# An attention-then-MLP kernel: the second quarter of the weights asked for earlier in the opening, and the order of the first layer's tiles changed to suit

## The chip, the cores and the metric

The kernel runs on one core of a Trainium2 chip. The time is device microseconds (us) of one execution; the median of five executions before the change is 203.65 us (202.69 to 204.04).

## What is computed

```python
# q, k, v: (4 batches, 8 heads, 768 steps, 64), fp32
gamma = 1.0 - 2.0 ** (-5.0 - np.arange(H))
for t in range(S):
    state = gamma[None, :, None, None] * state + np.einsum('bhd,bhe->bhde', k[:, :, t], v[:, :, t])
    y[:, :, t] = scale * np.einsum('bhd,bhde->bhe', q[:, :, t], state)
x = y.transpose(0, 2, 1, 3).reshape(3072, 512)
h = x @ w_in                      # w_in: 512 x 2048
g = gelu_tanh(h)
return g @ w_out                  # w_out: 2048 x 512
```

A decaying linear attention gives 512 features for each of 3,072 tokens; a two-layer MLP follows.

## The kernel before

**Tiling.** The 768 steps are cut into six chunks c of 128. A chunk has four batches b, so 512 tokens. Within a chunk the attention of a batch is made of matmuls: q and k, cast to fp16 and scaled (`prep1`, line 147), are transposed on TensorE (`mm_T`, 184) and evicted to qkT (`ev_T`, 193); scores are formed (`mm_A`, 203) and masked on VectorE (`ev_A`, 217); `mm_yc` and `mm_yi` (224, 239) form y, and `ev_Y` (252) writes it to xT, the MLP's input; `mm_s` and `ev_S` (261, 275) update the state st that chunk 1 needs. In chunk 0 `mm_yc` issues nothing.

**First layer (M1).** The 2,048 hidden features are 16 tiles fc of 128. `moe1` (372) computes one tile for all 512 tokens: four matmuls and one GELU on ScalarE. `moe1_two` (377) computes the pair fp, tiles 2fp and 2fp+1, for a stretch of tokens: t01 is batches 0 and 1, t2 batch 2, t3 batch 3. Each uses one of the two PSUM banks of the tag h, so a third has to wait for the GELU of the first. In chunk 0 the first layer starts before all batches are there; that is why pairs are computed stretch by stretch.

**Weights.** w_in is loaded in four parts of four tiles (`load_w_in`, 329): part 0 holds pairs 0 and 1, part 1 pairs 2 and 3, part 2 pairs 4 and 5, part 3 pairs 6 and 7. w_out comes in four parts too (`load_w_out`, 337). All are cast from fp32 to fp16 by the DMA and are issued from the queue of GpSimd (POOL in the profile).

**Second layer of chunk 0** (`units_0`, 614; its matmuls are lines 624 and 657). Products of g with w_out and of sums of both (`g_sums`, 402, and `w_sums`, 395, on VectorE), so it needs w_out parts as they come. Chunk 1's attention is woven in: after unit 3 ScalarE casts the first q and k rows of chunk 1, and after unit 5 TensorE transposes them.

**What sets the order.** The scheduling is manual. Each engine works through its own instructions in the order of the program text, and an instruction that has to wait holds up all behind it on that engine, DMA issues included. DMA issues stand on three queues: SP (`nc.sync`), ACT (`nc.scalar`) and POOL (`nc.gpsimd`). The rows of chunk 0 are issued from SP and ACT (lines 96 to 106, 717, 718, 726). POOL casts the k rows of chunk 0 and issues w_in, w_out and eight loads of chunk 1's rows:

```python
    prep1(PO, "k", 0, 0)          # 721
    load_w_in(0)                  # 722
    ...
    prep1(PO, "k", 0, 1)          # 728
    ...
    prep1(PO, "k", 0, 2)          # 740
    for i in range(1, 3):
        load_w_in(i)
    prep1(PO, "k", 0, 3)          # 743
    load_w_in(3)
```

`spin` (115) issues matmuls on zeros. The opening of chunk 0 is lines 717 to 801; line 787 is a one-element copy that keeps a later load behind w_out part 3, and `hold` (470) is another of the same kind.

Of the kernel before, what the change touches and what calls it, by code (L numbers as in the profile page):

```python
# [16 lines left out]
def kernel(  # L17
# [9 lines left out]
    nc = tc.nc  # L27
# [6 lines left out]
    NF = d_ff // 128  # L34
# [34 lines left out]
    misc = const.tile([128, 32], F32)  # L69
# [9 lines left out]
    def ld_tile(nm, c, b):  # L79
        if (nm, c, b) not in raw:  # L80
            tag, n = ("v1" if nm == "v" else "qk1", 5 if nm == "v" else 8) if c == 1 else (f"{nm}32", 4)
            raw[nm, c, b] = ld.tile([128, H, Dh], F32, tag=tag, bufs=n, name=f"{nm}32")
        return raw[nm, c, b]

    def load1(eng, nm, c, b):
        eng.dma_start(  # L86
            out=ld_tile(nm, c, b),
            in_=srcs[nm][b, :, c * C:(c + 1) * C, :].rearrange("h p d -> p h d"),
        )

    def load(c):
# [20 lines left out]
        out=misc[:, 0:1], in_=zero[:, 0:1], func=AF.Gelu_apprx_tanh, scale=1.0  # L112
    )

    def spin(n):
        ps = bank("h", shape=(128, 512), name="spin_ps")
        for _ in range(n):
            nc.tensor.matmul(
                out=ps, lhsT=zero[:, 0:128], rhs=zero, start=True, stop=True
            )  # L120


    st = const.tile([128, B, NHP, 2, 64], F16, name="st")
# [4 lines left out]
    for j in range(2):  # L128
        for hp in range(NHP):
            nc.vector.tensor_scalar(  # L130
                out=mask[:, j, hp],
# [9 lines left out]
    def copy_on(eng, out, in_):  # L141
        if eng is nc.scalar:
            eng.copy(out=out, in_=in_)  # L143
        else:
            eng.tensor_copy(out=out, in_=in_)

    def prep1(eng, nm, c, b):
        if nm == "v":
            t = pre.tile([128, H, Dh], F16, tag="v16", bufs=6, name="v16")
        else:  # L150
            if (c, b) not in qk16:
                qk16[c, b] = pre.tile([128, 2, H, Dh], F16, tag="qk16", bufs=6, name="qk16")
            t = qk16[c, b][:, "qk".index(nm)]
        src = ld_tile(nm, c, b)
        if (nm == "v") == (c < 1):
            copy_on(eng, t, src)
        else:
            col = OQ if nm == "q" else OK
            eng.tensor_tensor(  # L159
                out=t,  # L160
                in0=src,
                in1=cst[:, col:col + H].unsqueeze(2).broadcast_to([128, H, Dh]),
                op=ALU.mult,
            )
        h16[nm, c, b] = t
# [11 lines left out]
    def bank(tag, dt=F32, shape=(128, NHP, 128), name="ps"):  # L177
        return psum.tile(list(shape), dt, tag=tag, bufs=BANKS[tag], name=name)
# [5 lines left out]
    def mm_T(c, b):  # L184
        ps = bank("att", F16, (128, 2, NHP, 128), "qkT_ps")
        for i, nm in enumerate("qk"):
            for hp in range(NHP):
                nc.tensor.transpose(  # L188
                    out=ps[:, i, hp], in_=pair(h16[nm, c, b], hp), identity=iden
                )  # L190
        pss["T", c, b] = ps

    def ev_T(c, b, eng=nc.vector):
        copy_on(eng, qkT_tile(c, b), pss.pop(("T", c, b)))
# [8 lines left out]
    def mm_A(c, b):  # L203
        t = qkT[c, b]
        ps = [bank("att", name=f"a_ps{j}") for j in range(2)]
        for hp in range(NHP):
            for j in range(2):
                nc.tensor.matmul(  # L208
                    out=ps[j][:, hp],
                    lhsT=t[j * 64:(j + 1) * 64, 1, hp],  # L210
                    rhs=t[j * 64:(j + 1) * 64, 0, hp],
                    start=True,
                    stop=True,
                )
        pss["A", c, b] = ps

    def ev_A(c, b):
        ps = pss.pop(("A", c, b))
        for j in range(2):
            s = att.tile([128, NHP, 128], F16, tag=f"a{j}", bufs=2, name=f"a_sb{j}")  # L220
            nc.vector.tensor_tensor(out=s, in0=ps[j], in1=mask[:, j], op=ALU.mult)  # L221
            a_sb[c, b, j] = s
# [29 lines left out]
    def ev_Y(c, b, eng=nc.vector):  # L252
        if c not in xT:
            xT[c] = xp.tile([128, NHP, B * C], F16, tag="x", bufs=2, name="xT")
        x, ps = xT[c][:, :, b * C:(b + 1) * C], pss.pop(("Y", c, b))
        if c < 1:
            copy_on(eng, x, ps)
        else:
            nc.vector.tensor_tensor(out=x, in0=ps, in1=dec, op=ALU.mult)  # L259
# [15 lines left out]
    def ev_S(c, bs, engs=(nc.vector, nc.vector)):  # L275
        if c + 1 >= NCk:
            return
        s_ps = pss.pop(("S", c, bs))
        for j in range(2):
            sl = slice(j * 64, (j + 1) * 64)  # L280
            t = st[sl, bs[0]:bs[-1] + 1, :, j]
            if c == 0:
                copy_on(engs[j], t, s_ps[sl])
                continue
            for hp in range(NHP):
                nc.vector.scalar_tensor_tensor(  # L286
                    out=t[:, :, hp],
                    in0=t[:, :, hp],
                    scalar=cst[sl, OG + hp:OG + hp + 1],
                    in1=s_ps[sl, :, hp],  # L290
                    op0=ALU.mult,
                    op1=ALU.add,
                )
# [32 lines left out]
    NO = 4  # L326
    w_out_sb = [const.tile([128, NF // NO, d_model], F16, name=f"w_out{i}") for i in range(NO)]

    def load_w_in(i):
        nc.gpsimd.dma_start(  # L330
            out=w_in_sb[i],
            in_=moe_w_in.rearrange("(kc p) n -> p kc n", p=128)[
                :, :, w_in_at[i] * 128:(w_in_at[i] + w_in_n[i]) * 128
            ],
        )

    def load_w_out(i):
        n = NF // NO
        nc.gpsimd.dma_start(
            out=w_out_sb[i],  # L340
            in_=moe_w_out.rearrange("(fc p) n -> p fc n", p=128)[:, i * n:(i + 1) * n],
        )
# [4 lines left out]
    def moe1_mm(c, fc, out, t0, t1):  # L347
        wi, wr = w_in_of[fc]
        for kc in range(NHP):
            nc.tensor.matmul(  # L350
                out=out,
                lhsT=w_in_sb[wi][:, kc, wr * 128:(wr + 1) * 128],
                rhs=xT[c][:, kc, t0:t1],
                start=(kc == 0),
                stop=(kc == NHP - 1),
                skip_group_check=True,
            )

    def g_tile(c, fc):
        r = fc % 8 // 2 * 2  # L360
        return g_sb[fc // 8][:, r:r + 2]
# [7 lines left out]
    def gelu(out, in_):  # L369
        nc.scalar.activation(out=out, in_=in_, func=AF.Gelu_apprx_tanh, scale=1.0)  # L370

    def moe1(c, fc):
        h_ps = bank("h", shape=(128, B * C), name="h_ps")
        moe1_mm(c, fc, h_ps, 0, B * C)
        gelu(g_tile(c, fc)[:, fc % 2], h_ps)

    def moe1_two(c, fp, t0, t1):

        h_ps = bank("h", shape=(128, 2, B * C // 2), name="h_ps")
        for r in range(2):  # L380
            moe1_mm(c, 2 * fp + r, h_ps[:, r, 0:t1 - t0], t0, t1)
        gelu(g_tile(c, 2 * fp)[:, :, t0:t1], h_ps[:, :, 0:t1 - t0])
# [320 lines left out]
    def loads(eng, c, *what):  # L703
        for nm, b in what:
            load1(eng, nm, c, int(b))
# [7 lines left out]
    VE, AC, PO, SY = nc.vector, nc.scalar, nc.gpsimd, nc.sync  # L713
# [12 lines left out]
    load1(AC, "k", 0, 3)  # L726
    prep1(VE, "q", 0, 1)
    prep1(PO, "k", 0, 1)
    spin(2)
    mm_A(0, 0)  # L730
    ev_A(0, 0)
# [6 lines left out]
    ev_Y(0, 0, AC)  # L738
    prep1(VE, "q", 0, 2)
    prep1(PO, "k", 0, 2)  # L740
    for i in range(1, 3):
        load_w_in(i)
    prep1(PO, "k", 0, 3)
    load_w_in(3)
    for i in range(NO):
        load_w_out(i)
    loads(PO, 1, "q0", "k0", "q1", "k1", "v0", "v1", "q2", "k2")
    mm_A(0, 1)
    ev_A(0, 1)
    spin(2)  # L750
# [8 lines left out]
    mm_A(0, 2)  # L759
    ev_A(0, 2)  # L760
    ev_S(0, (0, 1), (AC, VE))
    prep1(VE, "q", 0, 3)

    t01, t2, t3 = (0, half), (half, half + C), (half + C, 2 * half)
# [2 lines left out]
    mm_yi(0, 2)  # L767
    ev_Y(0, 2, AC)
    moe1_two(0, 1, *t01)
    prep1(AC, "v", 0, 3)  # L770
    mm_T(0, 3)
    ev_T(0, 3)
    moe1_two(0, 0, *t2)
    moe1_two(0, 1, *t2)
    mm_A(0, 3)
    ev_A(0, 3)
    moe1_two(0, 2, *t01)
    mm_yc(0, 3, "o")
    mm_yi(0, 3)
    mm_s(0, (2, 3))  # L780
    ev_Y(0, 3)
    ev_S(0, (2, 3))
    moe1_two(0, 2, *t2)
    for fp in range(3):
        moe1_two(0, fp, *t3)

    nc.gpsimd.tensor_copy(out=dec[0:1, 0, 0:1], in_=w_out_sb[3][0:1, 0, 0:1])
# [1 line left out]
    loads(PO, 1, "q3", "k3", "v2", "v3")  # L789
    loads(SY, 2, *[x + str(b) for nm in ("qk", "v") for b in range(B) for x in nm])  # L790

    for fc in range(6, NF):
        moe1(0, fc)
        if fc == 7:
            g_sums(VE, 0, 0, 2)
            w_sums(0)
        if fc == 8:
            g_sums(VE, 0, 2, 4)
        if fc == 11:
            w_sums(1)  # L800
            g_sums(VE, 0, 4, 6)
# [262 lines left out]
```

## Time and profile before

| what | value |
|---|---|
| median of five runs | 203.65 us |
| time of the profiled execution | 203.65 us |
| its span, first to last instruction | 200.8 us |
| granted TensorE clock, mean | 0.992 |
| PE busy | 190.6 us, 95% of the span |
| DVE, ACT, POOL busy | 133.8, 119.0, 132.2 us |
| DMA | 34.24 MB, mean 171 GB/s |
| w_in parts 0 to 3: issue | 6.63, 11.87, 12.68, 17.94 us |
| w_in parts 0 to 3: landing | 14.93, 20.31, 22.85, 25.39 us |
| batch 3's q, k, v: landing | 16.12, 16.36, 17.17 us |
| w_out part 0: landing | 27.96 us |

PE is TensorE's matmuls and PEld its weight loads, DVE is VectorE, ACT ScalarE, POOL GpSimd, SP the sync engine; a q behind a name means its sequencer. L350 is line 350. Times in the trace count from the span's start. A wait row names the engine and line that waited, what ended the wait, and the total, the number and the longest of the waits. A timeline row has the start, the duration, the engine, the line, the operation, its output and inputs, and in brackets the idle time before it with what ended it. In the chain of work that ended last, each step is followed back to what released it, so it shows what set the pace; a DMA in it is a transfer from its issue to its landing. A DMA queue's row has packets, megabytes and the time of its packets as a share of 16 engines over the window.

### The profile page before, as it was taken

The numbers are of one execution on the slowest core, as the hardware profiler recorded it, in microseconds if no ns is written. First come the engines' busy times: TensorE is split into PE (matmuls) and PEld (weight loads), VectorE is DVE, ScalarE is ACT, GpSimd is POOL, SyncE is SP. The second block draws the span as 40 slices with busy tenths as digits, with TensorE's granted clock in tenths as the row PEclk, the third lists the DMA queues.
The fourth block names the chain that finished last, engine by engine and source line by source line (L and its number), as shares of the span: only waits on it lengthen the run. The fifth ranks groups of instructions, "written<-read, shape, count | busy, mean of one in ns | idle before, by whom it ended". The sixth has DMA issues, their size and how long they took to land.

```text
span 200.8 us, 5015 instructions
## 1 busy us (share of the span) xinstructions
PE 190.6 (95%) x2014; PEld 149.1 (74%) x2014; DVE 133.8 (67%) x279; ACT 119.0 (59%) x218; POOL 132.2 (66%) x134
## 2 busy tenths in 40 slices
PE   5588999999999999999999999999999999999993
PEld 1346746887888888745478887888888888888882
DVE  5356759869792449995997975995835935217720
ACT  2386474473589409265657698379584495867211
POOL 0557833845189998769969529389979299598100
PEclk9889999999999999999999999999999999999999
DMA  7999999999998799999999597531400220002204
GB/s 164 288 235 227 206 207 242 343 341 218 322 238 119 175 259 213 175 295 248 216 221 253 132 246 173 119 151 48 108 0 3 97 112 3 0 0 109 104 25 184
DMA packets 87094, 34.24 MB, mean 171 GB/s; under 512 B 80032, under 2 KB 84512, under 8 KB 87072
## 3 DMA queue, kind: packets, MB, share of 16 engines
q1 hardware_dynamic: 73920, 19.25, 45.0%
q0 software_dynamic: 6624, 12.58, 24.0%
q10 hardware_dynamic: 6528, 2.10, 4.1%
q8 instruction: 15, 0.25, 0.5%
q14 instruction: 7, 0.06, 0.1%
HBM read 27.63 MB, written 6.29 MB: 169 GB/s over the span
## 4 chain that ended last, share of the span: by engine, by line
PE 86%; DMA 8%; DVE 2%; SPq 1%; POOL 1%; issue 1%; ACT 0%; DVEq 0%
PE o_ps L504 31%; PE h_ps L350 19%; PE h_ps L586 19%; DMA w_in<-in_moe_w_in_dram 4%; DMA k<-in_k_dram 3%; PE y_ps L243 3%; PE o_ps L624 3%; PE a_ps L208 3%; PE o_ps L657 3%; PE y_ps L230 2%; PE s_ps L267 1%; SPq L86 1%; DVE a_sb L221 1%; PE qkT_ps L188 1%; DVE xT L259 1%; POOL qk L159 1%
## 5 line engine op out<-in xcount | busy, mean ns | idle before, releaser
L350 PE MATMUL h_ps<-xT,w_in 128*128 128x256 f16 (+2 forms) x304 | 45.9, 301 | 1.3 <-DMA w_in<-in_moe_w_in_dram 1.3
L370 ACT ACTIVATE g<-h_ps 128x512 f16<-128x512 f32 (+1 forms) x55 | 31.5, 577 | 20.4 <-PE h_ps L350 18.5
L221 DVE TENSOR_TENSOR a_sb<-a_ps,mask 128x512 f16<-128x512 f32 x48 | 30.5, 684 | 15.9 <-PE a_ps L208 13.3
L393 POOL TENSOR_TENSOR s_g<-g 128x512 f16<-128x512 f16 x30 | 35.2, 1180 | 7.5 <-ACT g L370 6.5
L350 PEld LDWEIGHTS <-w_in 128*128 128x128 f16 x304 | 26.5, 98 | 15.8 <-DMA w_in<-in_moe_w_in_dram 1.7
L504 PEld LDWEIGHTS <-s_g 128*128 128x128 f16 x320 | 30.7, 98 | 4.2 <-POOL s_g L393 0.3
L370 ACT ACTIVATE g<-h_sb 128x512 f16<-128x512 f32 x36 | 22.0, 634 | 17.4 <-DVE h_sb L393 17.0
L504 PE MATMUL o_ps<-t_w,s_g 128*128 128x256 f16 x240 | 29.4, 273 | 0.0
L393 DVE TENSOR_TENSOR h_sb<-h_ps,h_sb 128x512 f32<-128x512 f32 x36 | 22.9, 684 | 9.6 <-ACT h_sb L143 8.9
L159 POOL TENSOR_TENSOR v<-v,cst 128x512 f16<-128x512 f32 x20 | 20.6, 1046 | 5.4 <-DMA v<-in_v_dram 4.2
L504 PEld LDWEIGHTS <-g 128*128 128x128 f16 x208 | 20.2, 98 | 2.5
L393 POOL TENSOR_TENSOR s_g<-s_g,g 128x512 f16<-128x512 f16 x18 | 21.0, 1164 | 1.4
L393 POOL TENSOR_TENSOR s_g<-g,s_g 128x512 f16<-128x512 f16 x18 | 20.6, 1155 | 0.0
L586 PEld LDWEIGHTS <-t_in 128*128 128x128 f16 x192 | 18.0, 98 | 2.9
L143 ACT COPY h_sb<-h_ps 128x512 f32<-128x512 f32 x36 | 19.1, 598 | 1.3 <-PE h_ps L586 1.2
L504 PE MATMUL o_ps<-w_out,g 128*128 128x256 f16 x160 | 19.1, 273 | 0.0
L286 DVE SCALAR_TENSOR_TENSOR st<-st,cst,s_ps 64x128 f16<-64x128 f16 x64 | 18.2, 346 | 0.2
L586 PE MATMUL h_ps<-s_x,t_in 128*128 128x256 f16 x144 | 17.8, 273 | 0.0
L259 DVE TENSOR_TENSOR xT<-y_ps,dec 128x512 f16<-128x512 f32 x20 | 13.3, 684 | 5.4 <-PE y_ps L243 5.4
L586 PEld LDWEIGHTS <-w_in 128*128 128x128 f16 x144 | 14.1, 98 | 1.8
L143 ACT CAST qk<-q 128x512 f16<-128x512 f32 x20 | 12.6, 630 | 2.8 <-DMA q<-in_q_dram 2.8
L143 ACT CAST qk<-k 128x512 f16<-128x512 f32 x20 | 12.6, 630 | 0.1
(81 smaller groups left out, 263.2 us busy)
## 6 DMA issues: line engine op xcount, KB each, us to landing
out_dram<-o_sb POOLq DMA_DIRECT2D x10, 512.0 KB, 3.6
k<-in_k_dram SPq DMA_DIRECT2D x18, 256.0 KB, 4.5
q<-in_q_dram SPq DMA_DIRECT2D x18, 256.0 KB, 4.5
v<-in_v_dram SPq DMA_DIRECT2D x18, 256.0 KB, 4.4
w_in<-in_moe_w_in_dram POOLq DMA_DIRECT2D x4, 512.0 KB, 8.4
w_out<-in_moe_w_out_dram POOLq DMA_DIRECT2D x4, 512.0 KB, 11.9
q<-in_q_dram POOLq DMA_DIRECT2D x4, 256.0 KB, 11.0
k<-in_k_dram POOLq DMA_DIRECT2D x4, 256.0 KB, 9.5
```

What stands on the lines that cost most here:

```text
L143: eng.copy(out=out, in_=in_)
L159: eng.tensor_tensor(out=t, in0=src, in1=cst[:, col:col + H].unsqueeze(2).broadcast_to([128, H, Dh]), op=ALU.mult,)
L208: nc.tensor.matmul(out=ps[j][:, hp], lhsT=t[j * 64:(j + 1) * 64, 1, hp], rhs=t[j * 64:(j + 1) * 64, 0, hp], start=True, stop=True,)
L221: nc.vector.tensor_tensor(out=s, in0=ps[j], in1=mask[:, j], op=ALU.mult)
L243: nc.tensor.matmul(out=y_ps[j * 64:(j + 1) * 64, hp], lhsT=h16["v", c, b][:, 2 * hp + j], rhs=a_sb[c, b, j][:, hp], start=(c == 0), stop=True,
L259: nc.vector.tensor_tensor(out=x, in0=ps, in1=dec, op=ALU.mult)
L286: nc.vector.scalar_tensor_tensor(out=t[:, :, hp], in0=t[:, :, hp], scalar=cst[sl, OG + hp:OG + hp + 1], in1=s_ps[sl, :, hp], op0=ALU.mult, ...
L350: nc.tensor.matmul(out=out, lhsT=w_in_sb[wi][:, kc, wr * 128:(wr + 1) * 128], rhs=xT[c][:, kc, t0:t1], start=(kc == 0), stop=(kc == NHP - ...
L370: nc.scalar.activation(out=out, in_=in_, func=AF.Gelu_apprx_tanh, scale=1.0)
L393: eng.tensor_tensor(out=out, in0=in0, in1=in1, op=op)
L504: nc.tensor.matmul(out=po, lhsT=lhs(c, lk, fp, a), rhs=rhs(rk, fp), start=(new and fp == 0 and (last or a == 0)), stop=(stop and fp == NP ...
L586: nc.tensor.matmul(out=self.ps[G, k][:, p], lhsT=self.lhs(lk, 2 * G + p, kc), rhs=self.rhs(rk, kc), start=(new and p == 0 and kc == 0), st ...
```

## The change

It edits the opening of chunk 0 only.

- Part 1 of w_in is issued from POOL right behind the cast of batch 1's k.
- Parts 2 and 3 of w_in, the cast of batch 3's k, w_out and chunk 1's loads move down the POOL queue, behind a one-element copy that reads st after the state update of batches 0 and 1.
- On TensorE, pairs 0 to 3 (tiles 0 to 7) of M1 are computed on batches 0 to 2 around batch 3's transposes; before, only pairs 0 and 1 came ahead of batch 3's scores. Five pairs instead of three are then taken stretch by stretch, and six tiles instead of ten on all 512 tokens at once.
- VectorE's sums of g pairs and of w_out part 0 are placed behind tile 10 instead of tiles 7 and 8.

```diff
     prep1(VE, "q", 0, 1)
     prep1(PO, "k", 0, 1)
+    load_w_in(1)
     spin(2)
...
     prep1(VE, "q", 0, 2)
     prep1(PO, "k", 0, 2)
-    for i in range(1, 3):
-        load_w_in(i)
-    prep1(PO, "k", 0, 3)
-    load_w_in(3)
-    for i in range(NO):
-        load_w_out(i)
-    loads(PO, 1, "q0", "k0", "q1", "k1", "v0", "v1", "q2", "k2")
     mm_A(0, 1)
...
     ev_S(0, (0, 1), (AC, VE))
+    nc.gpsimd.tensor_copy(out=misc[0:1, 2:3], in_=st[0:1, 0, 0, 0, 0:1])
+    for i in range(2, 4):
+        load_w_in(i)
+    prep1(PO, "k", 0, 3)
+    for i in range(NO):
+        load_w_out(i)
+    loads(PO, 1, "q0", "k0", "q1", "k1", "v0", "v1", "q2", "k2")
     prep1(VE, "q", 0, 3)
...
     moe1_two(0, 1, *t01)
+    for fp in range(2):
+        moe1_two(0, fp, *t2)
+    for fp in range(2, 4):
+        moe1_two(0, fp, *t01)
     prep1(AC, "v", 0, 3)
     mm_T(0, 3)
     ev_T(0, 3)
-    moe1_two(0, 0, *t2)
-    moe1_two(0, 1, *t2)
+    for fp in range(2, 4):
+        moe1_two(0, fp, *t2)
     mm_A(0, 3)
     ev_A(0, 3)
-    moe1_two(0, 2, *t01)
+    moe1_two(0, 4, *t01)
     mm_yc(0, 3, "o")
     mm_yi(0, 3)
     mm_s(0, (2, 3))
     ev_Y(0, 3)
     ev_S(0, (2, 3))
-    moe1_two(0, 2, *t2)
-    for fp in range(3):
+    moe1_two(0, 4, *t2)
+    for fp in range(5):
         moe1_two(0, fp, *t3)
...
-    for fc in range(6, NF):
+    for fc in range(10, NF):
         moe1(0, fc)
-        if fc == 7:
+        if fc == 10:
             g_sums(VE, 0, 0, 2)
             w_sums(0)
-        if fc == 8:
             g_sums(VE, 0, 2, 4)
```

## The prediction

> **What bounds the kernel now.** I read the 40 slices first: PE is at 9 tenths from slice 8 to the last, so nothing outside the first 40 us can be won here, and the question is how much PE idles in the opening. The waits of PE between 13 and 33 us answer it:
>
> ```profile
> PE h_ps L350 <- DMA w_in<-in_moe_w_in_dram: 1.3, 2, 0.7
> PE qkT_ps L188 <- POOL qk L159: 0.5, 1, 0.5
> ```
>
> The columns are total us, times, longest. The first wait for w_in (0.65 us, at 14.97) is for part 0, which the change leaves alone. That leaves 0.69 us for part 1 (until 20.36) and 0.48 us for the cast of batch 3's k (until 18.05): 1.17 us in all can be removed.
>
> Then the chain that ended last, in order of time:
>
> ```profile
> 3.98 6.72 DMA k<-in_k_dram
> ...
> 10.76 1.11 POOL qk L159
> 11.87 8.44 DMA w_in<-in_moe_w_in_dram
> ...
> 20.36 1.05 PE h_ps L350 x8
> ...
> 23.63 9.26 PE h_ps L350 x48
> 32.90 5.24 PE o_ps L624 x48
> 38.14 0.45 PE qkT_ps L188 x8
> ```
>
> Up to 20.3 us the chain is DMA, behind it PE without a break. The timeline shows what stands close behind PE at 38 us, the casts on ACT of the first rows of chunk 1:
>
> ```profile
> 36.35 0.62 ACT L143 CAST qk<-q 128x512 f16<-128x512 f32 x1 [2.82 <-DMA q<-in_q_dram]
> ...
> 37.11 0.62 ACT L143 CAST qk<-k 128x512 f16<-128x512 f32 x1
> ...
> 37.97 0.61 PE L188 MATMUL qkT_ps<-iden,qk 128*128 128x128 f16 x8
> ```
>
> ACT starts each cast as the row lands (36.33, 37.09). The k cast ends at 37.73; PE's four transposes of k run at about 38.2. So if PE came earlier, it would stop here: with k ready at 37.73 and 0.3 us for the four, this step can end at 38.1 at best instead of 38.58. **The gain is capped at about 0.5 us** unless those rows land earlier. They cannot: in windows of 2 us the DMA share is 1.21 to 1.28 from 6 to 34 us without a hole and 1.02 to 1.06 on larger packets to 40 us, and the change removes no byte.
>
> How the queues share the engines, from 10.9 to 11.7 us:
>
> ```profile
> q0 software_dynamic: 159, 0.16, 121.7%
> q10 hardware_dynamic: 29, 0.01, 4.0%
> q1 hardware_dynamic: 2, 0.00, 0.5%
> ```
>
> and from 12.5 to 13.5 us:
>
> ```profile
> q0 software_dynamic: 138, 0.14, 82.8%
> q1 hardware_dynamic: 139, 0.04, 26.9%
> q10 hardware_dynamic: 116, 0.03, 13.1%
> ```
>
> The columns are packets, MB, share. q0 is POOL's (w_in, 512 packets of 1 KB a part), q1 is SP's and q10 ACT's (rows, 1,024 packets of 256 B each). First the weights alone at 200 packets a us, then nearly equal packet counts, so four times the bytes for w_in. From 14 to 15 us the rows alone move at 1,100 packets a us.
>
> **Part 1 of w_in moved ahead: where it lands.** POOL ends the cast of k1 at 9.12 and issues part 1 there (0.81 us, to 9.93) instead of at 11.87. The cast of k2 starts when k2 lands (10.69), so that issue costs nothing on POOL: it lies in a wait of 1.64 us. What it does at the engines is the open question. The Trainium skill ("DMA: Bandwidth & Descriptors", Queues, rings and completion order) says that each DMA engine goes round the queues that have work, packet by packet, and this speaks against the change: with 1 KB against 256 B, a second part of w_in takes most bytes from batch 3's rows. The 12.5 row agrees with it. But another row does not: part 0 was issued at 6.63, and between 7.6 and 10.5 no packet of q0 moved; an idle queue shows its first packet about 1.3 us after POOL's issue (store at 129.05, none before 130.36). Part 0 began only when the rows issued before it were through; part 1 began at about 16.0 when batch 3's rows were. Two readings then:
> - By the rule, part 1 follows part 0 in q0 and shares with the rows. At 12.5 us 184 packets of part 0 are left (512 less the 328 from 10.5 on), plus 512: 696 / 138 = 5.0 us, to 17.5. Part 0 landed 0.95 us after its bulk (14.0 to 14.93), part 1 1.56 us after it (18.75 to 20.31): landing 18.5 to 19.1, I take 18.8.
> - By the row, it stays behind all rows issued up to 9.43 and lands at 20.31 as now.
> I take the rule, because the equal counts come just where both kinds have been issued early; the row is the rival below.
>
> **Batch 3's rows.** By 17.5 us the rows have moved some 120 + 5.0 x 270 = 1,470 of their 3,072 packets; 1,600 are left, 1.45 us, to 19.0. q3 and k3 end at about 18.1 and, with the lag of 0.9 us that v3 shows now (bulk 16.25, landing 17.17), land at 19.0; v3 at 19.9 (now 16.12, 16.36, 17.17). The cast of k3 took 1.56 us, the others 1.03 to 1.17: ready at 20.1 to 20.6.
>
> **The hold.** A one-element copy (nearest row: POOL's 1x1 CAST, 0.18 us) waits for ACT's eviction of st, 14.76 to 15.34. Should it wait for DVE's half too, it is 16.37. Behind it on POOL stand parts 2 and 3, the cast of k3, w_out and chunk 1's loads. Parts 2 and 3 are then issued from 15.6 to 17.2 (latest 18.1). At about 16.9 only some 570 KB are ahead, all issued by 9.43; the engines need part 2 at 19.0, so there is no hole with a lag of 1.3 us either way. w_out is issued from about 20.6, needed at 24.1 (19.0 plus two parts of 2.55). The stream keeps its order and loses only the mixing: 696 of 1 KB at 200 and 1,360 of 256 B at 1,100 would take 4.7 us, the mix 5.0. So it is about 0.25 us later: part 2, now landing at 22.85 (4.1 after 18.75) lands at 19.0 + 4.1 = 23.1. Today nobody waits for part 2; then PE does.
>
> **The order on PE.** No matmul is added or removed. Pairs 0 and 1 of M1 on batches 0 and 1, and batch 2's y, end as now at 17.2. Their stretch of batch 2 (t2, 0.45 each) runs at 17.2 and, since the bank comes free with the GELU that ends at 17.98, at 18.0 to 18.5. Pairs 2 and 3 start with part 1 at 18.8 and take 1.75 (16 matmuls of 128x256 at 0.109), to 20.55; then batch 3's transposes (k cast ready in time or 0.1 late), t2 of pairs 2 and 3 (0.9) and the scores (0.35), to 22.3. Pair 4 needs part 2: **PE waits 0.8 us, to 23.1**. From there I take now's durations: pair 4 0.98, y and s 0.59, then six groups of t2 or t3 instead of four, 2.17 (21.93 to 24.10) plus 2 x 0.5, then six full tiles on all batches instead of ten, 6 x 0.863 = 5.18. Sum 9.92, so M1 ends at 33.0; now 32.73. The scores' eviction (1.29 on DVE) ends at 23.7, before it is needed at 24.1. DVE's sums of pairs 0 and 1 move from 24.1 to about 27, beside the wait for w_out 0 that DVE has now (2.3 us), and push its chain by 0.3 to 0.5; it ended 0.29 ahead of PE and still meets PE's +0.3.
>
> So the opening trades waits of 1.17 us for 0.4 (bank), 0.3 (part 1) and 0.8 (part 2). Sum: +0.3 us at 33.0, nothing later to absorb it (PE's two waits behind 21 us are 0.2 each). The profiled run's own time, 203.65 (span 200.8 and 2.85 around it), is also the median: **203.95**.
>
> **Rivals.**
> - *Part 1 stays behind the rows (the move does nothing), slower.* Pairs 2 and 3 start at 20.36, with 1.85 us idle since 18.5 because the work that fills it now has been put behind them. Then the scores end at 23.8, DVE's eviction at 25.15 holds y (0.45), and 0.59 + 3.17 + 5.18 follow: M1 ends at 34.1, +1.4: 205.0. M1 ends at landing + 13.7 whenever that is later than 33.0; it counts as slower from a landing at 20.0. For it: part 0's late start. Against: the equal counts. The clock could add to it: the Trainium skill ("TensorE: Matmul & The Clock Gate", What's actually happening) has it halved after an idle window. Here the window 4.65 to 8.06, with 1.21 us of PE busy, was followed by 0.50, and the others with 2.7 or more by 1.00; this rival would have 1.6 in 18.31 to 21.72. By the near row a window at half clock costs another 1.7. Chance 0.22.
> - *Part 2 overtakes v3.* If part 2 shares before the rows are through, v3 gets 36 KB a us beside two parts and lands at about 25: y waits, +2.2, 205.9. It counts from a landing at 24.1. The hold's 570 KB, issued 6 us before, speak against it. Chance 0.10.
> - *Faster, up to the cap.* Part 2 lands by 22.3 and the waits go: M1 0.5 earlier, and chunk 1's k cast stops it: 203.2. Over 0.5% below is only possible if the stream speeds up. Chance 0.08.
> - *The forecast*, 203.95, own range 203.4 to 204.6. Chance 0.60.
>
> **The numbers.** A change below 0.5% (1.0 us) cannot be told from none. Slower by more: both slow rivals and the upper edge of the forecast, 0.38. Faster by more: 0.05. Within: 0.57. For 8 in 10 the range goes from the cap, 203.1, past the first rival, 205.6.
>
> **What would show it.** Right: part 1 lands at 18.5 to 19.1, k3 near 19.0, v3 near 20; PE waits for w_in at pair 4 until about 23.1; the first o_ps of L624 at 33.0. Wrong: a wait for w_in until 20.3 ahead of pair 2; a wait for v3; a hole in the DMA share between 16 and 24 us; or chunk 1's first k cast ending before 37.5, which would lift the cap.

## The result, and the profile after

| | before | after |
|---|---|---|
| median | 203.5 us (80 runs) | 204.05 us (43 runs) |
| lowest | 202.42 us | 203.34 us |
| ratio to before, 95% interval | | 1.004 (1.0024 to 1.0055) |
| profiled execution, span | 203.65, 200.8 us | 204.11, 201.8 us |

The change costs 0.4%, about 0.8 us (0.5 to 1.1). The interval leaves out no change, and its upper end lies just above 0.5%, below which the prediction counts a change as none. Some executions of most kernels here lie 1.5% or more above their kernel's fastest; ratios leave them out, and the profiles of early_hold, split_only and half_work_T_late caught such executions, so their spans are not compared.

The waits of PE between 13 and 34 us, first in the profile of after, then in a second profile of the same kernel (after_again):

```profile
PE h_ps L350 <- ACT g L370: 0.2, 1, 0.2
```
```profile
PE h_ps L350 <- DMA w_in<-in_moe_w_in_dram: 0.8, 1, 0.8
PE h_ps L350 <- ACT g L370: 0.2, 1, 0.2
```

Both waits of before are gone, for part 1 and for the cast of k3. In the second profile PE waits 0.84 us for part 2 at pair 4, which is the trade that was forecast; in the first it does not, because M1 started at 16.08 and PE came to pair 4 at 23.45, just as part 2 had landed (23.40). These are the rows of after over two stretches:

```profile
7.93:14.76 6.83, 6.10 (x47) 3.27 (x46) 3.87 (x6) 3.14 (x5) 3.30 (x4) 0.50 1.25 247
14.97:33.80 18.83, 18.26 (x226) 13.27 (x225) 12.77 (x27) 12.69 (x26) 11.34 (x14) 1.00 1.22 201
```

Behind the length come the busy times of PE, PEld, DVE, ACT and POOL, the granted clock, the DMA share and GB/s. The clock was halved for 6.8 us before M1, and M1 began 0.62 us behind part 0's landing (15.46). Before had a halved clock from 8.06 to 11.48. The clock column of before_again has 1.00 throughout its opening, but its matmuls say otherwise:

```profile
10.56 1.06 PE L118 MATMUL spin_ps<-zero 128*128 128x512 f16 x2
13.94 0.59 PE L118 MATMUL spin_ps<-zero 128*128 128x512 f16 x2
```

Two matmuls of one form take 1.06 us and later 0.59, so the clock was halved there too, until about 13.4. In the four profiles in which it stayed halved beyond 14 us (after, after_again, late_hold, order_only) M1 began 0.6 to 0.8 us behind part 0's landing, in the other ten at most 0.15 behind it. part2_free, with the same opening as after, was back at full clock at about 10.2 (its pair of such matmuls takes 0.61 at 11.61), so the late start is no effect of the change. But both profiles of the changed kernel are of the late kind; how it runs from an earlier start is not shown.

The chain that ended last in after:

```profile
1.85 6.64 DMA k<-in_k_dram
...
8.57 1.37 POOL qk L159
...
19.41 2.35 PE h_ps L350 x24
...
23.50 0.57 issue
24.07 0.69 DVE a_sb L221
...
24.81 0.38 PE y_ps L243 x7
...
25.44 8.52 PE h_ps L350 x72
33.96 5.24 PE o_ps L624 x48
39.20 0.45 PE qkT_ps L188 x8
```

There is no w_in in it any more. In its place y of batch 3 waits for the masked scores: from pair 4 to the stretches behind y it is 1.92 us here and 1.58 in after_again. The first transposes of chunk 1 come 1.1 us later than before (38.14).

Behind them most profiles run alike: the span less the start of these transposes is 162.8 us in before (200.8 less 37.97), after (201.8 less 39.04), before_again, order_only, pair4_late and part2_free. There all is decided by when PE gets to them. It is not so in after_again, with 163.8 us. Its waits of PE between 90 and 100 us:

```profile
PE a_ps L208 <- DVE a_sb L221: 0.6, 2, 0.4
```

There PE waits until VectorE has masked earlier scores, and runs 1.0 us later from 95 us on. late_hold and part2_free_T_late lose 0.8 and 0.9 us at the same place, no profile with the loads of before does; why is open.

The casts that stood close behind PE before have moved with it:

```profile
37.60 0.62 ACT L143 CAST qk<-q 128x512 f16<-128x512 f32 x1 [3.00 <-DMA q<-in_q_dram]
...
38.35 0.62 ACT L143 CAST qk<-k 128x512 f16<-128x512 f32 x1
...
39.04 0.61 PE L188 MATMUL qkT_ps<-iden,qk 128*128 128x128 f16 x8
```

The k cast ends at 38.97 (37.73 before). Its row landed at 38.32 and, in the second profile, 38.34, against 37.09 and 37.59 in the two of before, so the stream of transfers is 0.7 to 1.2 us later, and PE again has no more than some 0.3 us in hand.

The open question of the forecast was how part 1 shares with batch 3's rows. The queues in after, from 15 to 17.5 us (packets, MB, share):

```profile
q0 software_dynamic: 338, 0.35, 80.9%
q1 hardware_dynamic: 338, 0.08, 26.0%
q10 hardware_dynamic: 337, 0.09, 15.4%
```

Equal packets from each queue, so w_in took two thirds of the bytes (0.35 of 0.52 MB) ahead of rows issued before it (SP's and ACT's last issues ended at 10.13 and 9.25, part 1's at 10.69). Part 1 landed at 19.27 and 18.67 in the two profiles, part 2 at 23.40 and 23.61, k3 at 19.70 and 19.23, v3 at 20.48 and 21.28.

### The profile page after: what moved, and what is told of

Same layout as the page of the kernel before. It is cut to its first block, busy times and chain, and to the rows that moved or that the text cites. A ratio compares the mean times of both kernels' runs of the same rounds, so it can differ in the third digit from the quotient of the medians.

```text
span 201.8 us, 5082 instructions
## 1 busy us (share of the span) xinstructions
PE 192.7 (95%) x2046; PEld 151.8 (75%) x2046; DVE 133.8 (66%) x279; ACT 119.4 (59%) x220; POOL 132.5 (66%) x135
## 4 chain that ended last, share of the span: by engine, by line
PE 90%; DMA 3%; DVE 2%; issue 1%; ACT 1%; POOL 1%; ACTq 1%; DVEq 0%
PE o_ps L504 31%; PE h_ps L350 20%; PE h_ps L586 19%; PE y_ps L243 4%; PE a_ps L208 4%; DMA k<-in_k_dram 3%; PE o_ps L624 3%; PE o_ps L657 3%; PE y_ps L230 2%; PE qkT_ps L188 2%; DVE a_sb L221 2%; PE s_ps L267 1%; PE spin_ps L118 1%; POOL qk L159 1%; DVE xT L259 1%
## 5 line engine op out<-in xcount | busy, mean ns | idle before, releaser
L370 ACT ACTIVATE g<-h_ps 128x512 f16<-128x512 f32 (+1 forms) x57 | 31.7, 562 | 19.5 <-PE h_ps L350 17.5
L350 PEld LDWEIGHTS <-w_in 128*128 128x128 f16 x336 | 28.5, 97 | 13.3 <-issue 0.5
L370 ACT ACTIVATE g<-h_sb 128x512 f16<-128x512 f32 x36 | 21.9, 633 | 17.5 <-DVE h_sb L393 16.1
L159 POOL TENSOR_TENSOR v<-v,cst 128x512 f16<-128x512 f32 x20 | 20.5, 1047 | 5.2 <-PE y_ps L243 3.1
L586 PEld LDWEIGHTS <-w_in 128*128 128x128 f16 x144 | 14.1, 98 | 1.8
L143 ACT CAST qk<-q 128x512 f16<-128x512 f32 x20 | 12.6, 630 | 3.0 <-DMA q<-in_q_dram 3.0
L143 ACT CAST qk<-k 128x512 f16<-128x512 f32 x20 | 12.6, 629 | 0.3
## 6 DMA issues: line engine op xcount, KB each, us to landing
q<-in_q_dram POOLq DMA_DIRECT2D x4, 256.0 KB, 10.4
```

The source lines that it names most:

```text
L159: eng.tensor_tensor(out=t, in0=src, in1=cst[:, col:col + H].unsqueeze(2).broadcast_to([128, H, Dh]), op=ALU.mult,)
L350: nc.tensor.matmul(out=out, lhsT=w_in_sb[wi][:, kc, wr * 128:(wr + 1) * 128], rhs=xT[c][:, kc, t0:t1], start=(kc == 0), stop=(kc == NHP - ...
L586: nc.tensor.matmul(out=self.ps[G, k][:, p], lhsT=self.lhs(lk, 2 * G + p, kc), rhs=self.rhs(rk, kc), start=(new and p == 0 and kc == 0), st ...
```

## The experiments

The theory going in: the removed waits come back as later rows and a wait for part 2, and the first row of chunk 1 caps any gain. The rivals: the loss is chance in the start of M1; it is all in the DMA order; or all in the order on PE.

**after_again, before_again.** Both kernels unchanged, for a second profile.

> The changed kernel once more, for a second profile. Theory: part 1 of w_in lands at 18.5 to 19.3, k3 at 19 to 19.7, part 2 at 23.0 to 23.5, and the first o_ps of L624 starts at 33.0 to 33.8. If M1 starts at about 15.0 this time (it started at 16.1 in the first profile), PE waits 0.5 to 1.0 us for w_in part 2 ahead of pair 4 and M1 ends no earlier than 33.0. Rival (the later start of M1 in the first profile is the whole loss and is chance): with a start at 15.0 there is no such wait and M1 ends at 32.7.

> The kernel before once more, for a second profile. Theory: M1 starts within 0.3 us of w_in part 0's landing and ends 17.3 to 17.8 later; the landing of part 0 and the clock up to 15 us vary from run to run without the change. Rival (the later start of M1, 16.1, comes with the change): M1 starts at 15.0 again.

Measured: after_again started M1 at 15.47, waited 0.84 us at pair 4 and ended M1 at 33.66. before_again started at 15.86, waited 0.59 for the cast of q3 and 0.2 for part 1 (landed 20.93) and ended M1 at 33.52 (first profile: 14.97, 32.73). So M1's start varies by 0.6 to 0.9 us in either kernel without any change of the program. What differs is what the opening does with an early start: in before, pair 2 starts within 0.05 us of part 1's landing in both profiles, and M1 ends 12.4 and 12.6 us after it; in after, pair 4 starts within 0.05 us of part 2's landing in both, and M1 ends 10.4 and 10.05 us after it. In these four profiles before ended M1 at 32.7 at the earliest and after at 33.7, which fits the lowest times, 202.42 and 203.34. In after PE came to pair 4 at that moment by itself, in after_again it waited.

**loads_only.** The DMA part alone, with the old order on PE:

```diff
     prep1(PO, "k", 0, 1)
+    load_w_in(1)
...
-    for i in range(1, 3):
-        load_w_in(i)
...
     ev_S(0, (0, 1), (AC, VE))
+    nc.gpsimd.tensor_copy(out=misc[0:1, 2:3], in_=st[0:1, 0, 0, 0, 0:1])
+    for i in range(2, 4):
+        load_w_in(i)
```

(the cast of k3, w_out and chunk 1's loads follow as in the change).

> The change's DMA order (part 1 early, the one-element copy, parts 2 and 3 behind it) with the old order on PE. Theory (packets shared in turn, so batch 3's rows are 2.7 us later): batch 3's transposes stand at 17.2 on PE and wait for k3's cast until 20.1 to 20.6 instead of 18.05; M1 ends at 34.3 to 34.8, +1.6 to +2.0 us over before. Rival (the DMA order costs nothing by itself): within 0.3 us of before.

Measured: 206.67 over four executions, ratio 1.0153 (1.0089 to 1.0216), +3.1 us. PE's waits from 13 to 37 us:

```profile
PE qkT_ps L188 <- DVE qk L159: 2.5, 1, 2.5
PE qkT_ps L188 <- POOL qk L159: 1.5, 1, 1.5
PE h_ps L350 <- DMA w_in<-in_moe_w_in_dram: 0.4, 1, 0.4
```

The transposes of batch 3 waited for q3 and then for k3, until 21.58: k3 landed at 20.41, 4 us later than in before. The direction is the theory's; the size is larger, because k3 came 1.4 us later than reckoned and the clock was halved from 21.87 to 25.29 after the 4 us of idle PE. The rival falls.

**order_only.** The other part alone: the change's text with the old block of POOL issues at its old place, `load_w_in(1)` behind the cast of k1 and the copy taken out.

> The change's order on PE and VectorE with the old DMA order. Theory: part 1 lands at 20.3 as before, pairs 2 and 3 wait for it from 18.5, 1.8 us; M1 ends at landing + 13.7 = 34.1, +1.4 us over before. Rival (the order by itself costs nothing, the loss is in the DMA order): within 0.3 us of before.

Measured: 206.09, ratio 1.0102 (1.0065 to 1.0139), +2.1 us (the forecast 1.4 lies at the lower end). In its profile part 1 landed at 20.68 and pair 2 waited for it:

```profile
PE h_ps L350 <- DMA w_in<-in_moe_w_in_dram: 1.1, 1, 1.1
```

M1 ended at 34.69, 14.0 us after part 1's landing (the forecast had 13.7). Either half of the change costs 2 to 3 us, and together 0.8: each needs the other, and together they come back almost to where they started.

**early_hold.** The copy reads batch 1's stretch of xT, not st:

```diff
     ev_Y(0, 1, AC)
+    nc.gpsimd.tensor_copy(out=misc[0:1, 2:3], in_=xT[0][0:1, 0, C:C + 1])
...
-    nc.gpsimd.tensor_copy(out=misc[0:1, 2:3], in_=st[0:1, 0, 0, 0, 0:1])
```

(with parts 2 and 3 and what follows them behind it).

> The changed kernel with the one-element copy reading batch 1's stretch of xT instead of st, so parts 2 and 3 of w_in are let go about 1 us earlier. Theory (the hold comes too late, the engines run dry for about 0.5 us between the rows' end and part 2, and pair 4 waits for part 2): no hole in the queue's packets between 18 and 21 us, part 2 lands at 22.9 to 23.1 instead of 23.4 to 23.6, and the time is 0.3 to 0.6 us under the changed kernel's: ratio to before 1.000 to 1.002. Rival (part 2 is late because of the sharing of packets alone): part 2 at 23.4 to 23.6 and a ratio of 1.004 as with the change.

Measured: median 209.35 of six executions (203.54 to 211.09, five of them at 208.49 or more); no ratio is formed from these. Both theories missed. Part 2 was issued at 14.08; with the copy on ScalarE's half of st it was 15.4 to 17.2 in the kernels here. The landing of v3 in the trace, and then the waits between 13 and 34 us:

```profile
DMA to landing us min/median/max: 18.3/18.3/18.3
```
```profile
PE h_ps L350 <- ACT g L370: 4.1, 2, 3.8
ACT v L143 <- DMA v<-in_v_dram: 3.9, 1, 3.9
```

v3 landed 18.3 us after its issue, at 26.09, between part 2 (23.19) and part 3 (26.40). ACT stood at v3's cast with the GELUs of M1 queued behind it, so PE stood for want of a PSUM bank. This has the form of the forecast's second rival, part 2 overtaking v3: the forecast had the landing (about 25) nearly right and the price (2.2 us) much too small, since it left out that ACT's whole queue stops.

That the earlier release causes it is not shown, though five executions of six speak for it. The profiles of split_only and half_work_T_late have the same stall with the loads of before. In split_only, ACT's wait, and the queues from 17 to 21 us:

```profile
ACT v L143 <- DMA v<-in_v_dram: 3.3, 1, 3.3
```
```profile
q0 software_dynamic: 796, 0.80, 120.4%
q1 hardware_dynamic: 40, 0.01, 1.9%
```

The last packets of v3 (q1) trickle in beside parts 1 and 2 of w_in (q0), and v3 lands at 21.82, 13.6 us after its issue. So there is a second way to a late v3, and what sets it off is open.

**late_hold.** The copy reads the half of st that VectorE evicts:

```diff
-    nc.gpsimd.tensor_copy(out=misc[0:1, 2:3], in_=st[0:1, 0, 0, 0, 0:1])
+    nc.gpsimd.tensor_copy(out=misc[64:65, 2:3], in_=st[64:65, 0, 0, 1, 0:1])
```

> The changed kernel with the one-element copy reading the half of st that VectorE evicts, some 1.0 us after ScalarE's half. Theory (the engines run dry before part 2, and part 2's landing sets M1's end): part 2 is issued 1.0 us later and lands at 24.3 to 24.6, pair 4 waits for it, M1 ends 0.7 to 0.9 us later than with the change, ratio to before 1.007 to 1.009. Rival (the release has slack): part 2 at 23.4 to 23.6 and ratio 1.004.

Measured: 205.13, ratio 1.0083 (1.0044 to 1.0122), as the theory had it, but not by its mechanism, so the match is luck. Part 2 was issued at 17.99 and landed at 23.70, 0.1 to 0.3 us later than with the change, and M1 ended at 33.75, no later. The time went behind M1. First come chunk 1's first rows, in the timeline:

```profile
39.52 0.40 PE L188 MATMUL qkT_ps<-iden,qk 128*128 128x128 f16 x4 [0.37 <-ACT qk L143]
39.61 0.62 ACT L143 CAST qk<-k 128x512 f16<-128x512 f32 x1
...
40.28 0.40 PE L188 MATMUL qkT_ps<-iden,qk 128*128 128x128 f16 x4 [0.36 <-ACT qk L143]
```

The whole stream behind part 2 is later (w_out part 0 29.41, k row 39.59), and PE waits twice for the casts and is 1.1 us later behind them; 0.8 us more went at 96 us, as in after_again. In after's own profile the engines ran partly dry; the DMA share from 18.5 to 20.5 us, in slices of 0.05 us:

```profile
DMA  9999999999999999637982648898998999999999
```

after_again shows none of it in the same stretch, and its part 2 still landed at 23.61. So part 2 is late without a hole too.

**pair4_late.** Pair 4 whole, behind the t3 stretches of pairs 0 to 3:

```diff
-    moe1_two(0, 4, *t01)
...
-    moe1_two(0, 4, *t2)
-    for fp in range(5):
+    for fp in range(4):
         moe1_two(0, fp, *t3)
...
-    for fc in range(10, NF):
+    for fc in range(8, NF):
```

> The changed kernel with pair 4 (tiles 8 and 9) taken whole behind the t3 stretches of pairs 0 to 3, so that PE needs part 2 of w_in 3 us later and one pair less is split. Theory (several floors lie close together): the wait for part 2 goes, but y of batch 3 now waits some 0.9 us for the masked scores, and chunk 1's k cast ends at 38.9 all the same; 0 to 0.4 us under the changed kernel, ratio to before 1.002 to 1.004. Rival (the wait for part 2 is the whole loss): 0.8 us less, ratio 1.000.

Measured: 205.3, ratio 1.0077 (1.0045 to 1.0109): worse, and both theories missed. PE's waits from 13 to 36 us:

```profile
PE h_ps L350 <- DMA w_in<-in_moe_w_in_dram: 2.2, 2, 1.4
PE y_ps L243 <- DVE a_sb L221: 1.2, 2, 0.8
PE h_ps L350 <- DVE xT L145: 0.5, 1, 0.5
```

The wait for part 2 went, but pair 4 had also been the cover for the masked scores (1.2 us) and for xT (0.5). 1.4 of the first row are for part 1, which landed at 20.0 in this profile; the edit does not touch part 1, so the profile does not say how much of the loss is the missing cover.

**half_work, half_work_T_late.** The cap, in the kernel before. The first halves the contraction of tiles 10 to 15 of chunk 0; the second also moves chunk 1's first transposes:

```diff
+        n = 2 if c == 0 and fc > 9 else NHP
-        for kc in range(NHP):
+        for kc in range(n):
...
-                stop=(kc == NHP - 1),
+                stop=(kc == n - 1),
...
-            5: [(att_T, 0)],
...
-            7: [(att_1A, 0)],
-            8: [(att_T, 1), (preps, 1, 2)],
+            7: [(att_T, 0)],
+            8: [(att_1A, 0), (att_T, 1), (preps, 1, 2)],
```

> The kernel before with half of the contraction of tiles 10 to 15 of chunk 0 left out (two matmuls of four each), so that M1 ends about 1.4 us earlier (then 0.63 us a tile by the GELUs). Theory (the gain in the opening is capped by the landing of chunk 1's first k row): PE waits at the transposes of chunk 1 until about 37.8 and the time falls by 0.4 to 0.6 us, ratio 0.997 to 0.998. Rival (no cap): 1.4 us less, ratio 0.993.

> The same with the first transposes of chunk 1 two units later in the second layer of chunk 0 (behind unit 7, their scores behind unit 8). Half of the contraction of tiles 10 to 15 of chunk 0 is left out here too. Theory (the cap is the place of these transposes): the wait goes and the time falls by 1.0 to 1.4 us, ratio 0.993 to 0.995. Rival (another limit, the landing of w_out or VectorE's sums, stands just behind): no more than 0.6 us, ratio 0.997 or above.

Measured: 202.47, ratio 0.9966 (0.9944 to 0.9987), and 202.22, ratio 0.9929 (0.99 to 0.9957): 0.7 and 1.4 us less. half_work's timeline has PE held by both casts:

```profile
37.24 0.40 PE L188 MATMUL qkT_ps<-iden,qk 128*128 128x128 f16 x4 [0.20 <-ACT qk L143]
37.34 0.62 ACT L143 CAST qk<-k 128x512 f16<-128x512 f32 x1 [0.15 <-DMA k<-in_k_dram]
...
38.01 0.40 PE L188 MATMUL qkT_ps<-iden,qk 128*128 128x128 f16 x4 [0.37 <-ACT qk L143]
```

In this profile M1 ended 1.1 us earlier than in before (31.64), and 0.9 of it was lost at these transposes. In the medians about half of the forecast 1.4 us is paid out, and all of it once the transposes stand later. The intervals overlap a little; the waits in the trace settle it. The cap is there, at 0.7 us by the median of half_work (0.3 to 1.1).

**part2_free, part2_free_T_late.** The change without its need for part 2 at pair 4, and the same with the later transposes:

```diff
-        wi, wr = w_in_of[fc]
+        wi, wr = w_in_of[fc - 4 if c == 0 and fc in (8, 9) else fc]
```

> The changed kernel with tiles 8 and 9 of chunk 0 computed from the weights of tiles 4 and 5, so that pair 4 needs part 1 of w_in and not part 2. Theory (the landing of part 2 sets M1's end, and the transposes of chunk 1 stand close behind): no wait for w_in at pair 4, M1 ends at 32.8 to 33.2, but chunk 1's k cast ends at 38.9 and holds PE; 0.2 to 0.4 us under the changed kernel, ratio to before 1.002 to 1.003. Rival (part 2 is the only floor): 0.8 us less, ratio 1.000. Second rival (part 2 is no floor): 1.004.

> The same (tiles 8 and 9 of chunk 0 from the weights of tiles 4 and 5) with the first transposes of chunk 1 two units later. Theory: both floors are away and the time falls 0.6 to 1.0 us under the changed kernel, ratio to before 0.999 to 1.001. Rival (a third limit, the sums on VectorE behind w_out): ratio 1.002 to 1.004.

Measured: 203.98, ratio 1.003 (1.0007 to 1.0053), and 204.32, ratio 1.0037 (1.0014 to 1.0061). The first is as expected and within its interval not apart from the change; the second is not: with both floors away the loss is still there, at the size that its rival named. part2_free's waits of PE from 13 to 34 us:

```profile
PE h_ps L350 <- DMA w_in<-in_moe_w_in_dram: 0.9, 2, 0.7
PE qkT_ps L188 <- POOL qk L159: 0.5, 1, 0.5
PE h_ps L350 <- ACT g L370: 0.2, 1, 0.2
PE y_ps L243 <- DVE a_sb L221: 0.2, 1, 0.2
PE qkT_ps L188 <- DVE qk L159: 0.2, 1, 0.2
```

M1 started at 14.90 and ended at 33.78, no earlier than after_again. k3 landed at 20.32, so batch 3's transposes waited 0.7 us for its and q3's casts; in part2_free_T_late 1.0 us (k3 at 20.39). In these two profiles the wait for k3 stands behind the wait for part 2. k3 came 0.6 to 1.2 us later in them than in the two of after, and part2_free_T_late also lost 0.9 us at 95 us, so how much of this holds in other executions is open. A wait for the rival's sums on VectorE stands in neither profile.

**split_only.** The kernel before, with no DMA moved and only pairs 3 and 4 taken by stretches:

```diff
-    for fc in range(6, NF):
+    for fp in (3, 4):
+        for t in (t01, t2, t3):
+            moe1_two(0, fp, *t)
...
+    for fc in range(10, NF):
         moe1(0, fc)
```

> The kernel before, with pairs 3 and 4 of M1 in chunk 0 taken by the stretches t01, t2 and t3 where it takes tiles 6 to 9 whole; no DMA is moved. It adds 32 matmul instructions as the change does, over the same columns. Theory (splitting itself costs): t2 and t3 stretches take 0.54 us each in the trace of the change and t01 0.9, so a pair takes 1.98 against 2 x 0.863 = 1.73 whole; two pairs 0.5 us, ratio 1.002 to 1.003. Rival (only columns count): ratio 1.000.

Measured: 203.81, ratio 1.0045 (1.0022 to 1.0067), +0.9 us. The rival falls, and the theory was too small. PE in the two pairs, at full clock:

```profile
27.41 1.93 PE L350 MATMUL h_ps<-xT,w_in 128*128 128x128 f16 x24
29.58 1.93 PE L350 MATMUL h_ps<-xT,w_in 128*128 128x128 f16 x24 [0.24 <-ACT g L370]
31.75 1.47 PE L350 MATMUL h_ps<-xT,w_in 128*128 128x128 f16 x12 [0.24 <-ACT g L370]
```

A row merges stretches of different length. Between the two waits lies one pair, t3 to t3: 2.17 us, against 1.73 for the same columns as two whole tiles; 0.44 more for each pair, 0.88 for two. 0.24 of each is a wait: the third stretch finds its bank still held by the GELU of the first.

## Why the prediction was right, step by step

The time was 203.95 forecast and 204.05 measured, and the range held. That they lie so close is partly luck: the forecast set out from 203.65, the median of before over many runs is 203.5, and the change costs 0.5 to 1.1 us where +0.3 was reckoned. The direction and the mechanism, waits traded for waits, were right.

- **Part 1 shares with the rows: right.** Equal packet counts; landing 18.8 forecast, 19.27 and 18.67 measured. Reading the rule of turns by packet of the Trainium skill ("DMA: Bandwidth & Descriptors", Queues, rings and completion order) over the late start of part 0 was the choice that mattered; order_only shows what the rival would have cost. PE came to pair 2 only at 19.85 and 19.24, so the 0.3 us of wait for part 1 fell away. The late start itself was read too simply: q3 and v2, whose issue began just before part 0's, landed at 16.12 and 11.64, when part 0 had been moving since 10.5. Parts 0 and 1 both began 3.9 to 4.1 us after their issue in before, so a lag of that size would explain them as well; no run tests it.
- **Batch 3's rows: right in kind, short in size.** k3 at 19.0 forecast, 19.2 to 20.4 measured over the kernels with these loads, v3 at 19.9 forecast, 20.5 and 21.3 measured in the change's two profiles.
- **Part 2 and the wait at pair 4: right in kind.** 23.1 forecast, 23.40 and 23.61 measured; 0.8 us of wait forecast, 0.84 in one profile, and none in the other, where PE came late by itself. The stream was to be 0.25 us later and was 0.7 to 1.2 later at chunk 1's k row.
- **"There is no hole": not always.** One of two profiles has one; part 2 landed no later in it than in the other.
- **"No matmul is added or removed": wrong as it stands, and yet the cost was in the sum.** 32 instructions are added (2,046 against 2,014 on PE). The sum took the stretches' durations from the trace: six groups of t2 or t3 at 3.17 us, measured 3.25 in both profiles. In after_again pairs 3 and 4 take 4.1 us by stretches, 0.6 more than as four whole tiles at 0.863. split_only's 0.9 us is larger because of a bank wait in each pair; the profiles of the change have one such wait in all (0.24 us, 0.4 forecast), ahead of pair 1's stretch of batch 2.
- **The cap: right.** half_work was held at the transposes as forecast.
- **M1's end: 33.0 forecast, 33.66 and 33.80 measured.** From the start of pair 4 the sum had 9.92 us, and after_again took 10.00. So the term that was too small there is the landing of part 2, by 0.5 us. In after it is that landing by 0.3 us and the wait of y for the masked scores (some 0.3 us), which the sum put at nothing because the scores were to end 1.1 us earlier than they did (22.3 against 23.43).
- **A reading that was wrong:** PE is at 9 tenths from the fifth of the 40 slices, 20 us, not from the eighth, and the last slice has 3. Nothing rests on it.

So of the 1.17 us that could be removed, the waits for k3 and part 1 are gone. By the trace of after_again 0.84 us came back at pair 4, 0.24 at a PSUM bank, and some 0.6 went into the splitting of two more pairs that the new order needs. That is an estimate of +0.5 us, the lower end of what was measured. The rest is not divided by these runs, because each cover or wait that is taken away exposes another wait behind it. No run with the whole work was faster than before.

## What to carry to other kernels

When an opening is fed by a saturated stream of transfers, asking for one transfer earlier can make another later, as here; look for who will wait for that one, and reckon with several waits standing a few tenths of an us behind the one in sight. Covering a wait by cutting work into smaller pieces has a price of its own, in PSUM banks and GELUs, and it is worth running alone before the cover is judged. Before any gain is booked, find the next place where an engine stands close behind the data: here that left an estimated 0.5 us to win, and half_work won 0.7.

## What the runs showed of the hardware that was not expected

- The issue of v3 took SP either 0.85 us or 1.5 to 1.8 us. With the loads of before, v3 landed at 17.0 to 18.0 in the three profiles with the longer issue (before, before_again, half_work) and at 19.8 to 22.5 in the three with the shorter (order_only, split_only, half_work_T_late). With the change's loads, k3 landed at 20.3 to 20.4 with the shorter issue (loads_only, pair4_late, part2_free, part2_free_T_late) and at 19.2 to 19.7 with the longer (after, after_again, late_hold; early_hold, with 20.25, does not fit). What decides between the two is open.
- A transfer of 256 KB in small packets, issued 6 us before two of 512 KB in packets of 1 KB, can still land behind the first and beside the second: 18.3 us from issue to landing in early_hold, 9.2 in before.
- The clock column can have 1.00 where the matmuls run at half speed (before_again, above). So a mean clock near 1.00 does not tell that an execution's opening ran at full clock; the durations of like matmuls do.
